# Two fused layers on one core: block 2's loads and score tiles, the value weights' place, and a new written order

## The chip, the cores and the metric

The kernel runs on one core of one Trainium2 chip. The metric is the device time of one execution in microseconds (us), from three runs. A core has TensorE (PE, matmuls; its weight loads are the row PEld), VectorE (DVE), ScalarE (ACT), GpSimd (POOL) and SyncE (SP). They run side by side, each its own instructions in the order written, and wait for each other by semaphores. Data moves by DMAs, which an engine issues and 16 DMA engines carry out.

## What is computed

```python
# first layer: q, k, v are (4 batches, 8 heads, 768 tokens, 64)
for t in range(S):
    state = gamma[h] * state + einsum('bhd,bhe->bhde', k[:, :, t], v[:, :, t])
    y[:, :, t] = scale * einsum('bhd,bhde->bhe', q[:, :, t], state)
# second layer: x is y as (4, 768, 512); x_prev is x one token earlier, zero at the start
xk = mu_k * x + (1 - mu_k) * x_prev
xr = mu_r * x + (1 - mu_r) * x_prev
k = maximum(xk @ w_k, 0)             # w_k (512, 1024)
v = k * k @ w_v                      # w_v (1024, 512)
out = v / (1 + exp(-(xr @ w_r)))     # w_r (512, 512)
```

## The kernel before

**Blocks.** The 3072 tokens are 12 blocks n of 256 tokens, three to a batch. Within a block the recurrence is done as attention: scores of the block's queries with its own keys, masked, times the values, plus the queries times the state that the blocks before left. Powers of gamma are folded into the values (`vs`), the state's decay (`G`) and a table `gy` by which the result is scaled.

**The order is written out by hand.** `ORDER` (L24) is a string of some 635 words, and L753 to L767 turn each word into instructions. A word is a code, its numbers (block first), `@` the PSUM banks that it uses, and `~` the engine: `v` DVE, `a` ACT, `p` POOL, `s` SP; without one it is a PE step. Each engine runs its own words in the order of the string. The words that matter here:

- `lq`, `lk`, `lv` load q, k, v of a block (L221). On POOL's queue they are cast to f16 for q and k. A split load (L227) is two DMAs. `wk.h`, `wv.h` load half of a weight matrix, `wr` the whole of w_r. `cq`, `ck` cast the first four heads of block 0, which SP's queue brings as f32.
- `gy.0`, `gy.1` build the table (L714; DVE). `cm` makes five constant masks: the identity for the transposes, two for 64-row score tiles, two others (L673).
- `Tq`, `Tk` transpose q and k on PE (L271 for blocks 0 to 3); `Eq`, `Ek` copy them out of PSUM. `S` makes scores, `M` masks them (L353, DVE), `C` the state's new part, `U` adds it up (L418), `G` decays it, `I` and `J` multiply queries by the state (L440), `Y` scores by values, `D` scales the result into xT (L513).
- `t` (ACT) and `X` (DVE, L551 for block 0) mix each token with its forerunner; `dx` is the difference that `X` uses for other blocks. `X.n.0.*` is for w_k, `X.n.1.*` for w_r.
- `K` are the matmuls with w_k (L581, L571), `Qa` and `Qb` relu and square (ACT), `R` those with w_r (L611), `s` the sigmoid, `V` those with w_v (L623), `O` the product, `st` the store. `Vc`, `Oc`, `sc` do the last 128 tokens in two halves (L641, L648).
- `z.12` is three f32 matmuls on zeros (L701), `z.1` and `z.2` one and two f16 ones of 128x512 (L708). Nothing reads their result.

**Three ways to make scores.** Blocks 6 to 11 (`HALF`) use 64-token tiles. Blocks in `WIDE` use tiles of 64 rows by 128 columns: `S` is 8 matmuls for each half of the tokens (L330), `Y` 16 (L477), with the `J` part apart, and `C` 8 for a batch's last block (L383). The others use 64x64 tiles: 16 for each half (L338), 32 and the `J` part inside `Y` (L488), 16 for `C` (L394). k and v of `WIDE` and `HALF` blocks are loaded split, since those take token p beside token p+128; the others take tokens 2p and 2p+1, which lie side by side in memory.

Of the kernel before, what the change touches and what calls it, by code (L numbers as in the profile page):

```python
# [12 lines left out]
ALU = mybir.AluOpType  # L13
# [70 lines left out]
def kernel(  # L84
# [12 lines left out]
    nc = tc.nc  # L97
    B, H, S, D = q.shape
# [3 lines left out]
    C = 128  # L102
# [99 lines left out]
    def wide(n):  # L202
        return n in WIDE

# [465 lines left out]
        for m in (1 << l for l in range(7)):  # L670
            nc.vector.tensor_scalar_add(out=count[:, m : 2 * m], in0=count[:, 0:m], scalar1=float(m))

    def masks(e):  # L673
        for out, col, op in (
            (ident, 0, ALU.is_equal), (causal[:, 0], 1, ALU.is_ge), (causal[:, 1], 1, ALU.is_gt),
            (step, 2, ALU.is_ge), (below, 0, ALU.is_ge),
        ):
            nc.vector.tensor_scalar(
                out=out, in0=count[:, 0 : out.shape[-1]], scalar1=mark[:, col : col + 1], scalar2=None, op0=op
            )  # L680

# [56 lines left out]
    def load_wv(e, h):  # L738
# [59 lines left out]
```

## Time and profile before

| what | value |
|---|---|
| median of 3 runs | 154.19 us (154.06 to 155.18) |
| the profiled execution | 154.38 us |
| its span, first to last instruction | 152.6 us |
| busy: PE, DVE, ACT, POOL | 144.1, 128.7, 100.6, 55.3 us |
| moved by DMA | 22.16 MB |

The page's first parts give busy times and, in 40 slices of 3.8 us, busy tenths (9 is 90% or more); PEclk is the clock that TensorE was granted. The chain follows the work that ended last back to the start; in order of time, its columns are start, duration, engine, tile, line and count. In the timeline a row is start, duration, engine, line, operation, output and input, count, and in brackets how long the engine was idle before and what released it. In the table by stretches, each engine has busy time and count.

### The profile page before, as it was taken

How to read it: one execution, taken by the hardware profiler on the slowest of the kernel's cores; microseconds unless marked ns; L12 is line 12 of the kernel's file. 1: busy time of each engine (PE TensorE's matmuls, PEld its weight loads, DVE VectorE, ACT ScalarE, POOL GpSimd, SP SyncE). 2: the span in 40 equal slices, each digit the busy share in tenths (PEclk: the TensorE clock that was granted, in tenths of full speed). 3: DMA queues.
4: the chain of work that ended last, by engine and by line, in shares of the span. 5: the costliest groups of instructions: out<-in, count | busy, mean ns of one | idle time of the engine just before them, and what ended most of it. 6: DMA issues, size and time to landing. Idle time of an engine off the chain costs nothing.

```text
span 152.6 us, 5532 instructions
## 1 busy us (share of the span) xinstructions
PE 144.1 (94%) x2426; PEld 82.9 (54%) x2426; DVE 128.7 (84%) x214; ACT 100.6 (66%) x187; POOL 55.3 (36%) x65
## 2 busy tenths in 40 slices
PE   7977799999999999999999999899999999999990
PEld 3354487758655554547554655557555445744450
DVE  7876999999999999999999999999789999702240
ACT  3466979899934894979483889879405048997130
POOL 7954988579867109997600000000000000000000
PEclk9999999999999999999999999999999999999999
DMA  5999999999999999999999203220002050010435
GB/s 137 215 224 200 207 229 194 170 249 210 196 167 207 236 250 112 290 275 203 206 191 225 83 0 136 81 73 0 4 4 75 0 205 1 14 54 4 158 117 206
DMA packets 45624, 22.16 MB, mean 145 GB/s; under 512 B 37400, under 2 KB 41248, under 8 KB 45600
## 3 DMA queue, kind: packets, MB, share of 16 engines
q0 software_dynamic: 38704, 14.42, 74.0%
q1 hardware_dynamic: 6592, 7.21, 13.7%
q8 instruction: 19, 0.31, 0.8%
q10 hardware_dynamic: 304, 0.18, 0.5%
q14 instruction: 5, 0.04, 0.1%
HBM read 24.16 MB, written 6.29 MB: 200 GB/s over the span
## 4 chain that ended last, share of the span: by engine, by line
PE 91%; DVE 3%; ACT 2%; issue 1%; DVEq 0%
PE ps L623 27%; PE ps L581 14%; PE ps L611 14%; PE ps L571 14%; PE ps L701 4%; PE ps L277 3%; PE ps L440 2%; PE ps L271 2%; DVE a L353 2%; PE ps L330 1%; PE ps L477 1%; ACT qT L240 1%; PE ps L317 1%; PE ps L461 1%; PE ps L641 1%; PE ps L365 1%
## 5 line engine op out<-in xcount | busy, mean ns | idle before, releaser
L623 PE MATMUL ps<-wv,k2s 128*128 128x512 f16 x184 | 43.3, 380 | 0.0
L590 ACT ACTIVATE kr<-ps 128x512 f32<-128x512 f32 x48 | 27.4, 596 | 21.5 <-PE ps L581 11.1
L623 PEld LDWEIGHTS <-k2s 128*128 128x128 f16 x184 | 17.0, 98 | 19.3 <-ACT k2s L602 0.2
L629 DVE SCALAR_TENSOR_TENSOR os<-ps,rs 128x512 f32<-128x512 f32 x23 | 15.5, 685 | 12.4 <-ACT rs L617 7.1
L611 PE MATMUL ps<-wr,xr 128*128 128x512 f16 x96 | 23.5, 379 | 0.0
L581 PE MATMUL ps<-xk,wk 128*128 128x256 f16 x192 | 23.4, 273 | 0.0
L571 PE MATMUL ps<-xk,wk 128*128 128x512 f16 x96 | 22.9, 379 | 0.0
L229 POOL DMA_DIRECT2D k<-in_k_dram x20 | 17.9, 908 | 11.1 <-PE ps L383 6.8
L581 PEld LDWEIGHTS <-wk 128*128 128x128 f16 x192 | 18.3, 98 | 4.4 <-issue 0.2
L240 ACT COPY qT<-ps 128x1024 f16<-128x1024 f16 (+1 forms) x13 | 12.4, 951 | 9.2 <-PE ps L277 7.8
L557 DVE SCALAR_TENSOR_TENSOR xr<-dx,mu,xT 128x256 f16<-128x256 f32 (+1 forms) x32 | 18.0, 579 | 0.1
L617 ACT ACTIVATE rs<-ps 128x512 f32<-128x512 f32 x24 | 13.7, 594 | 6.1 <-DVE os L629 3.2
L229 POOL DMA_DIRECT2D v<-in_v_dram x18 | 16.0, 904 | 3.6 <-DMA wr<-in_moe_w_r_dram 1.9
L557 DVE SCALAR_TENSOR_TENSOR xk<-dx,mu,xT 128x256 f16<-128x256 f32 (+1 forms) x32 | 17.1, 581 | 0.2
L353 DVE TENSOR_TENSOR a<-ps,c_sb 128x1024 f16<-128x1024 f32 (+1 forms) x14 | 14.6, 1066 | 0.7 <-PE ps L338 0.4
L602 ACT ACTIVATE k2s<-kr 128x512 f16<-128x512 f32 x24 | 14.6, 626 | 0.2
L571 PEld LDWEIGHTS <-wk 128*128 128x128 f16 x96 | 9.1, 98 | 10.3
L611 PEld LDWEIGHTS <-xr 128*128 128x128 f16 x96 | 9.1, 98 | 10.2 <-DVE xr L557 0.3
L598 ACT ACTIVATE k2s<-kr 128x512 f16<-128x512 f32 x24 | 14.4, 625 | 0.3
L240 ACT COPY kT<-ps 128x1024 f16<-128x1024 f16 (+1 forms) x13 | 12.3, 944 | 2.9 <-PE ps L271 2.0
L528 DVE TENSOR_TENSOR dx<-xT 128x1024 f32<-128x1024 f32 x11 | 13.5, 1223 | 0.3
L252 DVE TENSOR_TENSOR vs<-v,csm_sb 128x1024 f16<-128x1024 f32 x10 | 12.2, 1219 | 0.2 <-DMA v<-in_v_dram 0.2
(74 smaller groups left out, 165.5 us busy)
## 6 DMA issues: line engine op xcount, KB each, us to landing
out_dram<-os SPq DMA_DIRECT2D x23, 256.0 KB, 3.0
v<-in_v_dram POOLq DMA_DIRECT2D x18, 256.0 KB, 7.3
q<-in_q_dram POOLq DMA_DIRECT2D x11, 256.0 KB, 7.8
k<-in_k_dram POOLq DMA_DIRECT2D x21, 128.0 KB, 8.9
v<-in_v_dram POOLq DMA_DIRECT2D x2, 512.0 KB, 7.1
wk<-in_moe_w_k_dram POOLq DMA_DIRECT2D x2, 512.0 KB, 11.2
wv<-in_moe_w_v_dram POOLq DMA_DIRECT2D x2, 512.0 KB, 9.7
wr<-in_moe_w_r_dram POOLq DMA_DIRECT2D x1, 512.0 KB, 9.3
```

The lines of the kernel that those rows point to most:

```text
L229: e.dma_start(out=dst[:, :, i * D : i * D + D], in_=src[:, i * P : i * P + P].rearrange("h p d -> p h d"),)
L240: e.copy(out=out, in_=in_)
L353: nc.vector.tensor_tensor(out=a_full(n)[:, i, :, j0:j1], in0=pairs(banks("S", n, i, j0))[:, :, j0:j1], in1=(below if wide(n) else causal[: ...
L557: nc.vector.scalar_tensor_tensor(out=XM[w](k)[:, j, t0:t1], in0=DX(k)[:, j, t0:t1], scalar=mu[:, w * NCO + j : w * NCO + j + 1], in1=x[:, ...
L571: nc.tensor.matmul(banks("K", n, g), lhsT=wk16[:, co, g * P : g * P + P], rhs=XM[0](k)[:, co, :], start=(co == 0), stop=(co == NCO - 1),)
L581: nc.tensor.matmul(pz[:, i, :], lhsT=wk16[:, co, fo * P : fo * P + P], rhs=XM[0](k)[:, co, m * TM + t0 : m * TM + t1], start=(i == 0 and c ...
L590: nc.scalar.activation(out=kr, in_=banks("K", n, g, *u), func=AF.Relu)
L598: nc.scalar.activation(out=k2s[:, n % 3 : n % 3 + 2, g, :], in_=kr, func=AF.Square,)
L602: nc.scalar.activation(out=K2(n)[:, w * g : w * g + w, t0:t1], in_=kr.rearrange("p a t -> p (a t)").rearrange("p (i t) -> p i t", i=w), fu ...
L611: nc.tensor.matmul(banks("R", n, tb), lhsT=XM[1](k)[:, co, t : t + P], rhs=wr16[:, co, :], start=(co == 0), stop=(co == NCO - 1),)
L623: nc.tensor.matmul(banks("V", n, tb), lhsT=K2(n)[:, fo, tb * P : tb * P + P], rhs=wv16[:, fo, :], start=(fo == 0), stop=(fo == NFO - 1),)
L629: nc.vector.scalar_tensor_tensor(out=OS(2 * n + tb), in0=banks("V", n, tb), scalar=1.0 / (KSC * KSC), in1=RS(2 * n + tb), op0=ALU.mult, op ...
```

## The change

- `WIDE` loses block 2, so that its k and v are one DMA each, with its scores, values and state in 64x64 tiles, and `J.2` goes into `Y.2`.
- `masks` takes a part, so that the five masks can be placed in three words.
- `ORDER` is another. At the start: `gy.0` stands before the masks; `cq`, `ck` and `Ek.0.2.4` move from ACT to DVE, `U.0.0` from DVE to ACT; `lq.2` moves ahead of `wk.0`, and `wk.1` behind `vs.1` on POOL; `z.12 z.1 z.2` stay of `z.12 z.1` and five `z.2`; `Tq.2` comes ahead of the first `K`. Further on: `wv.0 wv.1` stand ahead of the loads of block 3, `vs.3` is on DVE where it was on POOL, `G.10` on ACT where it was on DVE, and PE's small steps stand in other groups between its large ones. Both orders end with `Vc.11.1.0 Oc.11.1.0 sc.11.1.0`.

```diff
-WIDE = (2, 3, 4, 5)
+WIDE = (3, 4, 5)
 ORDER = """
-cm gy.0~v mu~a lv.0~p lq.0.0.2~s lk.0.0.2~s ck.0.0.2~a cq.0.0.2~a z.12@6 Tq.0.0.2@0 Tk.0.0.2@1 gy.1~v
-z.1@2 mt@2 Ek.0.0.2~a Eq.0.0.2~a S.0.1.0.2@01 S.0.0.0.2@45 me~a lk.0.2.4~p Tk.0.2.4@2 Ek.0.2.4~a
-lq.0.2.4~p vs.0~v C.0@67 U.0.0~v Tq.0.2.4@3 Eq.0.2.4~a lq.1~p lk.1~p M.0.1.0.2~v z.2@2 S.0.1.2.4@23
-U.0.1~v lv.1~p lk.2~p I.0@01 S.0.0.2.4@67 M.0.0.2.4~v wk.0~p wk.1~p G.0~a z.2@6 Tq.1@6 Eq.1~a vs.1~p
-lq.2~p Tk.1@7 Ek.1~a M.0.0.0.2~v M.0.1.2.4~v Y.0 D.0~v t.0.0.3~a t.0.0.2~a t.0.0.1~a lv.2~p z.2@4
-S.1.1@23 M.1.1~v C.1@01 U.1.0~v z.2@4 I.1@23 S.1.0@67 X.0.0.1~v t.0.1.2~a X.0.0.2~v Tk.2@0 t.0.1.3~a
-t.0.0.0~a M.1.0~v X.0.0.0~v z.2@4 Y.1 t.0.1.1~a X.0.0.3~v Ek.2~a K.0.0@0 K.0.1@6 lq.4~p U.1.1~v
-G.1~a wr~p lk.4~p D.1~v dx.1~v X.1.0.2~v X.1.0.0~v K.0.2@1 Qa.0.0~a Qb.0.0~a Qa.0.2~a lq.3~p
...
-lq.11~p Tq.11@67 Ek.11~a X.8.1.2~v Tq.9@45 Eq.9~a K.6.1@0 Qa.6.1~a Eq.11~a R.6.0@2 s.6.0~a K.6.7@4
...
+lv.0~p lk.0.2.4~p mu~a gy.0~v cm.2~v lq.0.2.4~p lq.0.0.2~s cq.0.0.2~v cm.0~v z.12@6 Tq.0.0.2@0
+Eq.0.0.2~a lk.0.0.2~s ck.0.0.2~v Tk.0.0.2@1 Ek.0.0.2~a mt@0 S.0.0.0.2@23 cm.1~v Tk.0.2.4@1 lq.1~p
+vs.0~v C.0@45 gy.1~v Tq.0.2.4@6 Eq.0.2.4~a M.0.0.0.2~v me~a U.0.0~a Ek.0.2.4~v U.0.1~v G.0~a
+S.0.1.0.2@23 M.0.1.0.2~v lk.1~p lv.1~p S.0.0.2.4@67 Tq.1@4 Eq.1~a I.0@01 S.0.1.2.4@23 lk.2~p lq.2~p
+M.0.0.2.4~v Tk.1@5 M.0.1.2.4~v Y.0 D.0~v Ek.1~a t.0.0.3~a S.1.0@23 wk.0~p M.1.0~v vs.1~p Tk.2@5
+C.1@01 U.1.0~v z.1@6 I.1@23 t.0.1.1~a Ek.2~a X.0.0.3~v t.0.0.2~a t.0.0.1~a t.0.0.0~a U.1.1~v
+S.1.1@67 M.1.1~v X.0.0.0~v X.0.0.1~v G.1~a X.0.0.2~v wk.1~p Tq.2@5 t.0.1.0~a Eq.2~a z.2@4 Y.1 D.1~v
+dx.1~v X.1.0.2~v X.1.0.1~v t.0.1.2~a K.0.1@6 Qa.0.1~a t.0.1.3~a Qb.0.1~a K.0.0@7 Qa.0.0~a K.0.2@6
+X.1.0.0~v Qa.0.2~a Qb.0.2~a K.0.3@2 Qa.0.3~a lv.2~p S.2.1@45 lq.4~p X.1.0.3~v K.1.3@6 Qa.1.3~a
+vs.2~v S.2.0@23 Tq.4@01 X.1.1.0~v X.1.1.2~v C.2@7 U.2.0~v X.1.1.1~v wr~p K.1.2@6 Eq.4~a K.1.1@7
+Qa.1.2~a X.1.1.3~v lk.4~p M.2.1~v M.2.0~v I.2@01 R.1.0@6 s.1.0~a R.1.1@4 Qb.0.0~a K.1.0@6 wv.0~p Y.2
+X.0.1.2~v wv.1~p Tk.4@23 X.0.1.3~v Qa.1.0~a X.0.1.0~v Qb.0.3~a Qb.1.0~a X.0.1.1~v R.0.1@6 R.0.0@5
+lv.3~p D.2~v dx.2~v X.2.1.0~v X.2.0.2~v X.2.0.0~v X.2.0.1~v Qb.1.2~a s.0.0~a V.0.0.0@0 V.0.1.0@5
...
-    def masks(e):
+    def masks(e, part):
         for out, col, op in (
-            (ident, 0, ALU.is_equal), (causal[:, 0], 1, ALU.is_ge), (causal[:, 1], 1, ALU.is_gt),
-            (step, 2, ALU.is_ge), (below, 0, ALU.is_ge),
-        ):
-            nc.vector.tensor_scalar(
+            ((ident, 0, ALU.is_equal),),
+            ((causal[:, 0], 1, ALU.is_ge), (causal[:, 1], 1, ALU.is_gt)),
+            ((step, 2, ALU.is_ge), (below, 0, ALU.is_ge)),
+        )[part]:
+            e.tensor_scalar(
```

More of the change, by code (lines that the diff above doesn't have):

```diff
@@ new lines @@
+X.1.0.0~v Qa.0.2~a Qb.0.2~a K.0.3@2 Qa.0.3~a lv.2~p S.2.1@45 lq.4~p X.1.0.3~v K.1.3@6 Qa.1.3~a
[3 more added lines that the diff above has]
+lv.3~p D.2~v dx.2~v X.2.1.0~v X.2.0.2~v X.2.0.0~v X.2.0.1~v Qb.1.2~a s.0.0~a V.0.0.0@0 V.0.1.0@5
+Qa.1.1~a Qb.1.3~a s.0.1~a X.2.0.3~v V.0.1.1 O.0.1~v Ek.4~a lk.3~p K.2.2@1 V.0.0.1 vs.3~v X.2.1.1~v
@@ new lines @@
+Tk.7@23 V.1.1.0@5 V.1.1.1 V.2.0.1 X.3.0.3~v Ek.7~a G.4~a U.5.0~v st.0.0~s O.2.0~v O.2.1~v X.3.1.3~v
+K.3.1@2 K.3.0@4 Ek.5~a S.5.1@01 S.5.0@67 Qa.3.1~a Qa.3.0~a lq.9~p I.5@23 K.3.4@4 Qa.3.4~a lv.7~p
+Qb.3.0~a O.1.1~v lk.6~p K.3.6@5 Qa.3.6~a K.3.3@4 M.5.1~v J.5 Qb.3.1~a Qa.3.3~a M.5.0~v Tk.6@67
+Ek.6~a S.7@01 K.3.7@5 lq.6~p lv.6~p X.3.1.2~v X.3.1.0~v st.2.1~s Qb.3.4~a K.3.2@4 X.3.1.1~v Qb.3.6~a
+Qa.3.7~a Qa.3.2~a M.7~v R.4.1@6 s.4.1~a K.3.5@0 vs.6~v Qb.3.3~a C.6@45 Tq.6@67 vs.7~v Y.5 D.5~v
+U.6.0~a U.6.1~v U.6.2~v U.6.3~v Qa.3.5~a Qb.3.5~a Qb.3.2~a Qb.3.7~a R.3.1@1 dx.5~v X.5.1.3~v
@@ new lines @@
+X.5.0.1~v lv.11~s st.1.1~s R.3.0@0 s.3.0~a V.3.1.0@2 V.3.1.1 s.3.1~a O.3.1~v V.4.1.0@1 V.4.1.1
+X.5.1.2~v G.6~a X.5.0.2~v X.5.0.0~v Eq.6~a I.6@23 C.7@67 S.6@45 M.6~v X.5.0.3~v lq.8~p V.3.0.0@0
+U.7.0~v U.7.1~v V.3.0.1 O.3.0~v K.5.3@4 Qa.5.3~a K.5.1@5 X.5.1.0~v U.7.2~v Qa.5.1~a K.5.2@0 Qa.5.2~a
+Qb.5.2~a I.7@45 X.5.1.1~v Y.6 st.3.0~s st.2.0~s O.4.1~v K.5.0@6 Qa.5.0~a Qb.5.0~a U.7.3~v R.4.0@7
+s.4.0~a D.6~v dx.6~v R.5.1@6 s.5.1~a Qb.5.1~a lq.10~p Tq.10@23 lv.8~p vs.8~v Y.7 D.7~v dx.7~v
+X.6.1.1~v G.7~a Qb.5.3~a X.6.0.3~v X.6.0.2~v X.6.0.0~v lk.8~p Tk.8@01 Ek.8~a Eq.10~a V.5.1.0@6
@@ L80 @@
+X.11.1.0~v R.10.0@3 Qb.9.5~a Qa.11.0~a X.11.1.2~v R.9.1@1 R.11.0@2 Qb.9.6~a Qa.9.7~a st.7.0~s
+Qb.9.7~a s.9.0~a V.9.0.0@4 V.9.0.1 O.9.0~v V.10.1.1 V.9.1.0@6 Qb.11.0~a s.9.1~a Qb.11.1~a V.9.1.1
+O.9.1~v st.9.1~s st.9.0~s s.10.1~a O.10.1~v st.10.1~s R.11.1@4 Qa.11.2~a Qb.11.2~a s.11.1~a
+Vc.11.1.1@7 Oc.11.1.1~v V.11.0.0@4 V.11.0.1 sc.11.1.1~a s.10.0~a V.10.0.0@5 s.11.0~a O.11.0~v
+st.11.0~s V.10.0.1 O.10.0~v st.10.0~s Vc.11.1.0@2 Oc.11.1.0~v sc.11.1.0~s
 """
```

70 lines of the change are left out of this document (24 added, 46 removed).

## The prediction

> **What bounds the kernel now.** I read the page's first parts, then the chain of waits in order of time, then the timeline of the first 21 us and the loads.
>
> ```profile
> span 152.6 us, 5532 instructions
> ...
> PE 144.1 (94%) x2426; PEld 82.9 (54%) x2426; DVE 128.7 (84%) x214; ACT 100.6 (66%) x187; POOL 55.3 (36%) x65
> ...
> PE   7977799999999999999999999899999999999990
> ...
> DVE  7876999999999999999999999999789999702240
> ...
> PEclk9999999999999999999999999999999999999999
> DMA  5999999999999999999999203220002050010435
> ...
> PE 91%; DVE 3%; ACT 2%; issue 1%; DVEq 0%
> ```
>
> The reader is to see three things. PE's row is full from the sixth slice (19 us) to the end, so after 19 us only PE's own work and its few waits count. Ahead of that it shows 7s: this is the only stretch with time to win by order alone. DVE is also full from the sixth slice on, and the DMA engines up to 84 us, so PE's cover is thin there on both sides.
>
> ```profile
> 15.11 0.45 PE ps L338 x16
> ...
> 17.92 1.15 DVE a L353
> ...
> 19.11 0.64 PE ps L488 x32
> ...
> 19.86 3.60 PE ps L581 x32
> ...
> 26.26 0.55 PE ps L330 x16
> ...
> 29.15 0.59 PE ps L477 x16
> ...
> 53.24 0.97 PE ps L623 x4
> ...
> 58.56 0.86 PE ps L623 x4
> ...
> 95.67 0.45 issue
> ...
> 115.57 5.29 PE ps L623 x24
> ...
> 148.57 0.42 DVE os L648
> ```
>
> In this chain (start, duration, work) everything from 19.86 to 148.55 is PE, except 0.45 us of issue at 95.67, in the middle of a run of 64x64 transposes. 24 large matmuls take 5.29 us, 0.22 each. After small tiles a group of four takes 0.97 in place of 0.86, so each return from small to large costs 0.11; I take the same for going there.
>
> So the time is: the moment at which the first `K` can run (19.8 now), PE's work from there, PE's waits, and a tail (`Oc`, the last store) that both orders share. I cost each.
>
> **The first K.** These rows carry the walk.
>
> ```profile
> 3.11 1.62 DVE L678 TENSOR_SCALAR c_sb<-os,csm_sb 128x128 f16<-128x128 f32 x5
> ...
> 4.19 0.56 DVE L716 COPY gy_sb<-csm_sb 128x4 f32<-128x4 f32 x1
> ...
> 4.68 0.62 ACT L240 CAST k<-k2s 128x512 f16<-128x512 f32 x1 [2.01 <-DMA k2s<-in_k_dram]
> 4.78 2.57 DVE L726 TENSOR_TENSOR gy_sb<-gy_sb,csm_sb 128x4 f32<-128x4 f32 x8
> ...
> 7.53 1.23 DVE L252 TENSOR_TENSOR vs<-v,csm_sb 128x1024 f16<-128x1024 f32 x1 [0.18 <-DMA v<-in_v_dram]
> ...
> 9.44 0.42 DVE L242 CAST tg<-ps 128x256 f16<-128x256 f32 x1 [0.68 <-PE ps L394]
> ...
> 9.78 0.68 DVE L353 TENSOR_TENSOR a<-ps,c_sb 128x512 f16<-128x512 f32 x1
> ...
> 12.45 0.64 PE L271 MATMUL ps<-c_sb,q 128*64 128x128 f16 x16
> ...
> 13.58 1.90 POOL L252 TENSOR_TENSOR vs<-v,csm_sb 128x1024 f16<-128x1024 f32 x1 [3.90 <-DMA v<-in_v_dram]
> ...
> 14.26 1.23 DVE L513 TENSOR_TENSOR xT<-ps,gy_sb 128x1024 f32<-128x1024 f32 x1 [1.19 <-PE ps L440]
> ...
> 17.05 0.87 DVE L551 SCALAR_TENSOR_TENSOR xk<-xT,mu,dx 128x256 f16<-128x256 f32 x2
> ```
>
> DVE is free for its first new word at 3.11, as now. `gy.0` comes first: the rows from 4.19 to 7.35 are the copy and eight powers, 3.16 us, and the largest power, about 0.7, is `gy.1`; so `gy.0` takes 2.5, to 5.6. `cm.2` is two of the five masks that took 1.62, 0.6, to 6.2. The casts `cq`, `ck` are new on DVE. No row shows one from SBUF to SBUF: between 0.25 (half of what ACT takes, for a copy that no PSUM slows) and 0.7 (twice the 128x256 cast); I take 0.4, near that 0.42 row, since the source is SBUF. `cq` ends at 6.6, `cm.0` (the identity) at 6.9, and `Tq` starts there. Eight transposes take 0.4; ACT's two copies of 128x512 end near 8.45; the first `S` starts at 8.5. On DVE `ck`, `cm.1` end at 7.9; `vs.0`, whose load lands just ahead of its row's 7.53, at 9.1; `gy.1` at 9.75, the first `M` (0.65) at 10.4, `Ek.0.2.4` (0.55, as an `M`, bounded by 0.4 and 0.7) at 10.95. `U.0.1` waits for ACT's `U.0.0`, which stands behind `C.0` (9.55), `Tq.0.2.4`, its copy and `me`: 11.25. `U.0.1` ends at 11.65, three `M`s at 13.55, `Y.0` (0.64 and the state's part) at 14.4, `D.0` at 15.65, where it ends at 15.49 now.
>
> Behind `D.0` DVE does two large `M` (1.15 each), two `U` (0.35) and four `X` (0.4) before the first `K` may run; now it does the same but one `U`. That gives 20.3 against 19.8. With the short casts, masks of 0.2 and no wait of `U.0.1` it is 19.7; with the long casts, another copy of 0.7 and ACT late for `U.0.0` it is 21.2. I take 20.3. `C.1` hangs on POOL's `vs.1` at 13.58 to 15.48, whose load keeps its place in the queue, and is in time for `U.1.0` at 16.8.
>
> **PE's work from there.** `Tq.2` (0.64 by the row of 16) is done ahead of the first `K`, where it stands behind it now: -0.6. Block 2: `S` is 32 matmuls by the row of 16 in 0.45, 0.9, for 0.55: +0.35. `Y.2` is 0.64 for 0.59, and the eight `J` matmuls stay: +0.05. `C.2` is 16 small ones for 8: between 0 and +0.1, I take 0. Large matmuls are the same in number and shape. I count 25 groups of small steps between large ones from the first `K` on, for 24: +0.2. Sum 0.0. The removed `z.2` lie in idle time ahead of the first `K` and give nothing by themselves.
>
> **PE's waits.** The 0.45 at 95.67 falls in `Tk.11 Tq.11 Tq.9`, 96 transposes in one run; the new order has no run of three `T` so late. I count it as gone, between 0 and -0.45, and a new one is possible at any burst.
>
> **The loads.**
>
> ```profile
> 8.12 1.56 POOL L733 DMA_DIRECT2D wk<-in_moe_w_k_dram  x2
> ```
> ```profile
> wk<-in_moe_w_k_dram POOLq DMA_DIRECT2D x1, 512.0 KB, 10.3
> ```
> ```profile
> 19.75 1.83 POOL L229 DMA_DIRECT2D k<-in_k_dram  x2
> ...
> 30.61 0.78 POOL L740 DMA_DIRECT2D wv<-in_moe_w_v_dram  x1
> 31.76 0.75 POOL L740 DMA_DIRECT2D wv<-in_moe_w_v_dram  x1 [0.37 <-DMA q<-in_q_dram]
> ```
> ```profile
> k<-in_k_dram POOLq DMA_DIRECT2D x2, 128.0 KB, 9.4
> ```
> ```profile
> wv<-in_moe_w_v_dram POOLq DMA_DIRECT2D x1, 512.0 KB, 10.4
> ```
>
> `wk.0` lands at 18.4 now. `lq.2` ahead of it adds one load, and `k.2` as one DMA saves one issue, so about 18.7, against a need at 20.3. `wk.1` is issued behind `vs.1` at 15.5, just behind in the queue, lands near 21, and is needed by the third `K` at 22.1. Ahead of `wv.0` stand the same loads as ahead of `k.4`'s end now, which is at 30.1 (20.7 and 9.4). `wv.1` lands at 42.2 now (31.8 and 10.4); two halves there take about 2.5 each, so here they land near 32.5 and 35. From 20.3, eight `K` (0.9), four `R` and the small steps put `V.0.0.0` at 33.7 and the first use of `wv.1` at 35.5. `v.3` then lands near 37, when DVE reaches `vs.3`; `k.3`, `q.3` near 39 and 40, when PE reaches them. All just in time: cost 0 with little spare. `vs.3` on DVE is 1.2 us more there; its cover is `V.0.*` (four by 0.86), which PE now has ahead of `S.4`. With that cover gone it costs 1.2.
>
> **The sum.** Against the profiled execution: 154.38 + 0.5 (first `K`) + 0.0 (PE's work) - 0.45 (issue) = 154.43. The median of the three runs is 0.19 below that execution, so I predict 154.3: no change.
>
> **The rivals.**
>
> First, *the loads of block 3 come late* (slower). `vs.3` is in DVE's order, ahead of `X.2.1`, `O.0.0` and `M.4`; where `v.3` lands late, all of these wait, and PE soon after, since DVE has nothing spare:
>
> ```profile
> 8.00:12.00 4.00, 2.84 (x87) 1.93 (x87) 2.93 (x6) 2.59 (x9) 1.68 (x3) 1.00 1.61 241
> 12.00:16.00 4.00, 3.63 (x121) 2.33 (x121) 2.72 (x4) 2.35 (x4) 2.42 (x2) 1.00 1.70 188
> 16.00:20.00 4.00, 3.05 (x86) 1.87 (x87) 4.00 (x8) 3.38 (x8) 4.00 (x6) 1.00 1.37 202
> ...
> 36.00:40.00 4.00, 4.00 (x61) 3.20 (x58) 4.00 (x4) 3.94 (x8) 4.00 (x4) 1.00 1.25 206
> ```
>
> The columns are the stretch, its length, PE, PEld, DVE, ACT, POOL, clock and DMA. Two halves of `wv` ahead are 5 us of queue; I found about no spare, so being 1 to 3 us out costs 1 to 3. It decides from about 1.5 late. For it: DMA is full here. Against: `k.2` in larger pieces frees the queue a little. 155.4 to 157.4, say 156.4. Chance 0.24.
>
> Second, *the granted clock falls in the start* (slower). Eight of eleven f16 zero matmuls go. By my walk PE is busy some 3.1, 3.3 and 3.3 us of the three stretches above, against 2.84, 3.63 and 3.05, with no gap over 1 us; but it is small tiles now, and no row shows the clock without the zeros. If it is half from about 12 on, the small steps on the chain (`Y.0`, `S`, `I`, some 2 us) and the first `K`s (3.6 us) take up to twice as long: +2 to +5, say 157.5. It decides as soon as one slice from 4 to 7 has PEclk under 9. Chance 0.14. [...]
>
> Third, *the start is short and PE turns faster* (faster). The walk's lower end puts the first `K` at 19.7, -0.6. The other thing an order can change is what PE pays at the 25 groups: 0.11 going and 0.11 coming back. If tiles that follow each other better spared half of the returns (12 by 0.11), that is -1.3, and 154.3 - 0.6 - 1.3 = 152.4 at best; the first part alone gives 153.7. It needs nearly all of both to decide. For it: the new order has fewer long runs of small tiles. Against: as many groups as before. Chance 0.12.
>
> That the change does nothing of weight is the forecast itself.
>
> **How the numbers follow.** The forecast has 0.50, the late loads 0.24, the clock 0.14, the faster order 0.12. A difference of 1% (1.5 us) is about what a measurement of this kernel tells from no change. Faster by that: 0.12, the third. Slower: the clock 0.14, four fifths of the late loads 0.19 and the forecast's own upper end (first `K` at 21.2 with a new wait) 0.07, in all 0.40. Within: 0.48. The likeliest case alone runs from 153.5 to 155.3. The range takes in the better half of the faster order and the late loads and leaves out the worst of the clock: 152.9 to 157.4.
>
> **What would show it.** In the profile after: the first `K` (L582) within 19.7 to 21.2, `D.0` near 15.7, all PEclk 9; `vs.3` on DVE with no idle time ahead of it; no wait for a weight over 0.5; and L338 with 96 matmuls for 64, L330 with 48 for 64. PEclk under 9, DVE idle ahead of `vs.3`, or more than 2 us of PE waits after 21 us would make me wrong.

## The result, and the profile after

The changed kernel is slower: a median of 162.0 us (159.7 to 164.2, six runs) against 153.96 us of the kernel before on the same chip (153.78 to 155.18, six runs), a ratio of 1.045 with a 95% interval of 1.036 to 1.053. A ratio leaves out the runs that are more than 1.5% above the fastest of the same kernel, and a median counts all of them. The forecast was 154.3, and its range ended at 157.4. The profiled execution took 161.62 us. These are parts of its page that answer to those shown of before.

```profile
span 159.8 us, 5594 instructions
...
PE 147.5 (92%) x2458; PEld 85.3 (53%) x2458; DVE 130.9 (82%) x217; ACT 99.8 (62%) x188; POOL 51.7 (32%) x62
...
PE   7989879999999999992899979999999999999991
...
PEclk9987999999999999999569999999999999999999
...
PE 76%; DMA 10%; DVE 4%; ACT 4%; issue 2%; SPq 1%; ACTq 1%; DVEq 0%
```

PE's row has a hole in the 19th slice (a 2; 72 to 76 us), the granted clock is under 9 in two places (the third and fourth slice, and the two behind the hole), and the chain, which was 91% PE, now has 10% of DMA. The hole is read first, from the chain of waits in order of time (start, duration, what):

```profile
66.05 1.15 DVE vs L252
...
67.22 0.39 SPq L229
...
68.28 7.56 DMA out_dram<-os
...
75.97 0.70 DVE os L629
```

and from SP's waits (line, what it waited for: us in all, times, longest):

```profile
SPq L229 <- DVE vs L252: 8.5, 1, 8.5
```

SP's words here are `lv.11 st.1.1`. `lv.11` writes the buffer that `vs.7` (DVE, 66.05) still reads, so SP stands at it for 8.5 us, and `st.1.1`, whose data had long been ready, stands behind it. It is issued at 68.28, after the two loads of 256 KB, and lands 7.56 us later. `O.3.1` needs the output buffer that this store empties: there are four (`OS`, L152). In the order before, `lv.11` stands behind `st.3.1` (L57), and `st.1.1` goes out at 61.2; the list of changes ahead of the prediction does not have this move. What the late landing did to the engines, from the timeline:

```profile
75.97 0.69 DVE L629 SCALAR_TENSOR_TENSOR os<-ps,rs 128x512 f32<-128x512 f32 x1 [3.79 <-DMA out_dram<-os]
...
76.72 0.33 PE L440 MATMUL ps<-qT,tg 64*64 64x64 f16 x8 [3.70 <-DVE os L629]
...
77.93 3.60 PE L623 MATMUL ps<-wv,k2s 128*128 128x512 f16 x8
```

DVE, and through its PSUM bank PE, waits 3.7 us, and then eight `V` take 3.60 us where eight take 1.90 in the timeline of before: the clock has fallen.

```profile
93.45 1.90 PE L623 MATMUL ps<-wv,k2s 128*128 128x512 f16 x8
```

The table by stretches (length, busy and count of PE, PEld, DVE, ACT, POOL, then clock, DMA share, GB/s) shows it in both places:

```profile
72.00:76.00 4.00, 1.02 (x6) 0.33 (x5) 0.21 (x2) 0.35 (x1) 0.00 (x0) 0.94 1.38 281
76.00:80.00 4.00, 3.28 (x79) 1.88 (x79) 3.80 (x7) 0.00 (x0) 2.16 (x3) 0.50 0.66 45
...
10.00:12.00 2.00, 1.79 (x40) 1.46 (x41) 1.51 (x4) 1.51 (x8) 0.00 (x0) 0.67 1.33 303
12.00:14.00 2.00, 2.00 (x52) 1.66 (x52) 1.11 (x2) 1.74 (x4) 0.12 (x1) 0.50 1.73 188
```

In the trace's clock records, the half clock lasts 3.41 us from 10.67 and 6.83 us from 75.53, which is twice as long (and 10.24 us, three times, in a run below).

The start and the other waits, from the timeline and the chain:

```profile
14.49 1.23 DVE L513 TENSOR_TENSOR xT<-ps,gy_sb 128x1024 f32<-128x1024 f32 x1 [1.29 <-PE ps L440]
...
15.73 0.81 POOL L734 DMA_DIRECT2D wk<-in_moe_w_k_dram  x1
...
19.84 2.19 PE L581 MATMUL ps<-xk,wk 128*128 128x256 f16 x16
...
22.77 1.48 PE L581 MATMUL ps<-xk,wk 128*128 128x256 f16 x12 [0.74 <-DMA wk<-in_moe_w_k_dram]
```
```profile
15.73 6.99 DMA wk<-in_moe_w_k_dram
```
```profile
93.70 0.85 issue
```

The first `K` is at 19.84 (before: 19.79). PE's last instruction ends 7.7 us later than before (156.26 for 148.54), in four parts: 0.74 for `wk.1`, 3.70 for the store, about 2.6 of half clock behind that (an estimate; the eight `V` alone are 1.7 of it), and 0.4 more of issue wait (0.85 for 0.45); 0.3 is left, small steps. The tail behind PE is 0.5 shorter (3.6 for 4.1), which makes the span's 7.2.

### The profile page after: what moved, and what is told of

It is laid out like the page before. It is cut to its first block, busy times and chain, and to the rows that moved or that the text cites. A ratio compares the mean times of both kernels' runs of the same rounds, so it can differ in the third digit from the quotient of the medians.

```text
span 159.8 us, 5594 instructions
## 1 busy us (share of the span) xinstructions
PE 147.5 (92%) x2458; PEld 85.3 (53%) x2458; DVE 130.9 (82%) x217; ACT 99.8 (62%) x188; POOL 51.7 (32%) x62
## 4 chain that ended last, share of the span: by engine, by line
PE 76%; DMA 10%; DVE 4%; ACT 4%; issue 2%; SPq 1%; ACTq 1%; DVEq 0%
PE ps L623 21%; PE ps L571 13%; PE ps L581 12%; PE ps L611 12%; DMA out_dram<-os 6%; DMA wk<-in_moe_w_k_dram 4%; PE ps L702 3%; PE ps L277 3%; PE ps L440 3%; PE ps L271 2%; DVE os L629 1%; PE ps L317 1%; PE ps L365 1%; PE ps L461 1%; ACT rs L617 1%
## 5 line engine op out<-in xcount | busy, mean ns | idle before, releaser
L623 PE MATMUL ps<-wv,k2s 128*128 128x512 f16 x184 | 44.4, 390 | 0.0
L590 ACT ACTIVATE kr<-ps 128x512 f32<-128x512 f32 x48 | 28.0, 598 | 20.9 <-PE ps L581 13.4
L629 DVE SCALAR_TENSOR_TENSOR os<-ps,rs 128x512 f32<-128x512 f32 x23 | 15.5, 685 | 15.9 <-PE ps L623 10.4
L623 PEld LDWEIGHTS <-k2s 128*128 128x128 f16 x184 | 17.6, 100 | 20.3 <-issue 1.6
L617 ACT ACTIVATE rs<-ps 128x512 f32<-128x512 f32 x24 | 14.1, 595 | 20.3 <-DVE os L629 9.2
L581 PE MATMUL ps<-xk,wk 128*128 128x256 f16 x192 | 24.0, 276 | 0.9 <-DMA wk<-in_moe_w_k_dram 0.7
L571 PE MATMUL ps<-xk,wk 128*128 128x512 f16 x96 | 22.3, 379 | 0.0
L229 POOL DMA_DIRECT2D k<-in_k_dram x18 | 16.0, 907 | 8.1 <-PE ps L365 6.1
L229 POOL DMA_DIRECT2D v<-in_v_dram x16 | 14.4, 918 | 5.1 <-DMA wv<-in_moe_w_v_dram 3.5
L234 POOL DMA_DIRECT2D q<-in_q_dram x12 | 10.7, 891 | 16.6 <-PE ps L277 7.8
L252 DVE TENSOR_TENSOR vs<-v,csm_sb 128x1024 f16<-128x1024 f32 x11 | 13.3, 1215 | 0.1
```

Source lines behind the costliest of these rows:

```text
L229: e.dma_start(out=dst[:, :, i * D : i * D + D], in_=src[:, i * P : i * P + P].rearrange("h p d -> p h d"),)
L571: nc.tensor.matmul(banks("K", n, g), lhsT=wk16[:, co, g * P : g * P + P], rhs=XM[0](k)[:, co, :], start=(co == 0), stop=(co == NCO - 1),)
L581: nc.tensor.matmul(pz[:, i, :], lhsT=wk16[:, co, fo * P : fo * P + P], rhs=XM[0](k)[:, co, m * TM + t0 : m * TM + t1], start=(i == 0 and c ...
L590: nc.scalar.activation(out=kr, in_=banks("K", n, g, *u), func=AF.Relu)
L617: nc.scalar.activation(out=RS(2 * n + tb), in_=banks("R", n, tb), func=AF.Sigmoid, scale=1.0 / KSC)
L623: nc.tensor.matmul(banks("V", n, tb), lhsT=K2(n)[:, fo, tb * P : tb * P + P], rhs=wv16[:, fo, :], start=(fo == 0), stop=(fo == NFO - 1),)
```

## The experiments

Kernels marked "on the change" edit the changed kernel, those marked "on before" the kernel before. Ratios are to the kernel before on the same chip.

### The store

**The store ahead of the load** (on the change; the other kernels on the change named below with "the store ahead" contain this edit):

```diff
-X.5.0.1~v lv.11~s st.1.1~s R.3.0@0
+X.5.0.1~v st.1.1~s lv.11~s R.3.0@0
```

> One edit to the changed kernel: on SP's queue st.1.1 stands ahead of lv.11. Theory A: the changed kernel loses 3.7 us because st.1.1 stands behind lv.11, which waits until 67.2 us for vs.7, and then behind lv.11's data (it lands after 7.56 us, at 75.8), so that O.3.1, which needs the buffer, holds DVE and PE to 76; the granted clock then falls to half for 6.8 us, some 2.6 us more. With the store first, O.3.1 does not wait and the clock stays: 161.9 - 6.3 = 155.6 us, PEclk 9 after slice 5. Rival B: the DMA engines are so full at 68 to 76 us that stores land late wherever they stand: over 160 us, DVE still waits for out_dram. Rival C: DVE is behind by its own work there and the store only shows last: 158 to 160 us.

Measured: 156.76 us (155.91 to 158.03), ratio 1.015 (1.010 to 1.020). That is 5.2 us less by the medians and 4.6 by the ratios, from two words on one queue. SP's timeline, the clock's row on the page and two of PE's waits:

```profile
59.84 1.59 SPq L636 DMA_DIRECT2D out_dram<-os  x2
68.74 1.02 SPq L229 DMA_DIRECT2D v<-in_v_dram  x2
```
```profile
PEclk9955799999999999999999999999999999999999
```
```profile
PE ps L365 <- issue: 1.4, 1, 1.4
...
PE ps L277 <- issue: 0.6, 1, 0.6
```

Now both stores go before SP stands still, PE has no wait for a store, and the clock keeps full speed from there on: the fall at 76 followed from the wait. `st.1.1` is issued at 61.10 here and lands at 68.80 by the trace's landing records: 7.70 us with no load ahead of it on the queue. So it is not faster than in the changed kernel, only 7 us earlier. What is left over lies in the start, where this execution waited 1.97 us for the identity (to 7.44), ran at half clock for 10.24 us from 7.66 and reached the first `K` at 21.46, and in two issue waits, 0.64 at 68.36 and 1.35 at 89.56, where the changed kernel has one of 0.85. The 5.2 add up by that: 3.7 for the wait and 2.6 for the clock behind it, less 1.1 for the longer issue waits.

**A small load ahead of the store** (on the change; the loads of `lv.11` on SP bring only the first head of eight, so block 11's values are partly old data):

```diff
+            if split and n == NBLK - 1 and e is nc.sync:
+                hs = slice(0, 1)
             src = x[b, hs, t0 : t0 + TM, :]
```

> The changed kernel with lv.11 on SP's queue loading one head of eight (so block 11's values are partly old ones); its place, its wait for vs.7 and the order of st.1.1 behind it stay. Theory A1: of the store's delay the part that matters is lv.11's data ahead of it on the same queue: st.1.1 is still issued near 68.3 us but lands in 2 to 4 us, before O.3.1 is reached at 72: no DVE wait, no fall of the clock at 76, about 155.6 us. Theory A2: being issued as late as 68.3 is enough by itself: DVE still waits, over 159 us. Rival B (the other queues fill the DMA engines): the store still takes over 6 us, over 160 us.

Measured: 157.59 us (156.84 to 158.41), ratio 1.021 (1.017 to 1.026). The timeline:

```profile
75.63 0.69 DVE L631 SCALAR_TENSOR_TENSOR os<-ps,rs 128x512 f32<-128x512 f32 x1 [1.84 <-DMA out_dram<-os]
76.38 0.26 PE L442 MATMUL ps<-qT,tg 64*64 64x64 f16 x8 [1.74 <-DVE os L631]
```
```profile
69.35 6.16 DMA out_dram<-os
```

The wait is halved, 1.84 for 3.79, but the store still takes 6.16 us with an eighth of the data ahead of it, so the loads' data is at most 1.4 of the 7.56. Even that is not shown: in the run with zeros, next, the whole loads stand ahead and the store lands in 4.59 (69.66 to 74.25). What makes it late is that SP stands at `vs.7` for 8.5 us and issues it at 68.3 to 69.7 in place of 61. Why it then takes between 4.6 and 7.7 us, where the median of the stores is 2.3, is only argued: by the trace's packets POOL's loads moved 0.27 MB meanwhile in the execution of 4.59, and 0.80 to 0.99 MB in the three of 6.16 to 7.70. A wait of 1.74 did not make the clock fall behind it; one of 3.70 did. Length alone does not decide: in later runs it fell behind a wait of 3.00 and not behind one of 3.14.

**Zeros in the wait** (on the change; four f32 zero matmuls, eight records of PE in the trace, where PE waits for the store):

```diff
-G.6~a X.5.0.2~v X.5.0.0~v Eq.6~a I.6@23
+G.6~a X.5.0.2~v X.5.0.0~v Eq.6~a z.16@4 I.6@23
```

> The changed kernel with z.16 (four f32 matmuls on zeros, bank 4) ahead of I.6, that is in the 3.7 us in which PE waits for O.3.1. Theory A: the wait stays, but the granted clock does not fall at 75.5 us, so that the large matmuls after it take 0.22 us and not 0.44: 2 to 3 us less than the changed kernel, 159.2 us. Rival D: the half clock is hidden behind DVE and ACT, which have their own backlog after the wait: under 1 us less, 161 to 162 us.

Measured: 160.86 us (160.68 to 162.13), ratio 1.044 (1.040 to 1.049): in the total no difference that can be told from the changed kernel's. `O.3.1` in the timeline, and the stretches:

```profile
74.41 0.68 DVE L629 SCALAR_TENSOR_TENSOR os<-ps,rs 128x512 f32<-128x512 f32 x1
```
```profile
72.00:76.00 4.00, 4.00 (x18) 1.96 (x17) 3.95 (x8) 2.67 (x7) 2.06 (x3) 1.00 1.31 243
76.00:80.00 4.00, 4.00 (x87) 1.89 (x86) 0.79 (x2) 0.00 (x0) 0.59 (x1) 1.00 1.08 79
```

In this execution `O.3.1` did not wait for the store; the zeros themselves held PE, for 3.43 us, about as long as the wait of 3.70 that they were to fill. The clock holds behind them (1.00 for 0.50), and from the first `K` to PE's end it is 134.15 us for 136.42: 2.3 us less, although the issue waits are 0.7 longer (0.78 and 0.79 for 0.85). Less the 0.3 by which the zeros are shorter than the wait, that makes some 2.7 for the fall of the clock, near the estimate above. The total hides it, since this execution's start ran at half clock for 6.83 us and reached the first `K` at 21.30. The mean granted clock also differs from run to run (0.964 to 0.979 in these four); the next runs take up the start.

### The start

**Zeros back in the start** (on the change, with the store ahead; nine f16 zero matmuls, in groups of one and two, in PE's idle time before the first `K`):

```diff
-Ek.0.0.2~a mt@0 S.0.0.0.2@23
+Ek.0.0.2~a mt@0 z.1@7 S.0.0.0.2@23
-gy.1~v Tq.0.2.4@6 Eq.0.2.4~a
+gy.1~v Tq.0.2.4@6 z.2@7 Eq.0.2.4~a
-M.0.0.2.4~v Tk.1@5
+M.0.0.2.4~v z.2@5 Tk.1@5
-Y.0 D.0~v Ek.1~a
+Y.0 D.0~v z.2@4 Ek.1~a
-C.1@01 U.1.0~v z.1@6 I.1@23
+z.2@4 C.1@01 U.1.0~v z.1@6 I.1@23
```

> The changed kernel with st.1.1 ahead of lv.11, and with nine more f16 matmuls on zeros (z.1 and four z.2) in PE's idle time ahead of the first K. Theory G: the clock stays at full from 7 us on, the first K starts near 20 and not at 21.5, 1 to 1.5 us less than with the store first alone (156.8): 155.5 us. Rival H: the first K hangs on DVE's chain from csm_sb, and is late by that load: within 0.3 us of 156.8, with PEclk all 9.

Measured: 155.38 us (154.35 to 156.56), ratio 1.008 (1.005 to 1.011). The page's clock row, and PE's longest wait after the first `K`:

```profile
PEclk9999999999999999999999999999999999999999
```
```profile
PE ps L365 <- issue: 1.1, 1, 1.1
```

Work that computes nothing took 1.4 us off by the medians, 1.1 by the ratios. The mean granted clock is 0.995 to 1.0 in every run, where it was 0.967 to 1.0 without these zeros, and the first `K` is at 19.89. Not all of the 1.4 is the clock, though: with nine more matmuls ahead, the issue waits of 0.64 and 1.35 have become one of 1.10, which is 0.9 less, and the one run without these zeros that had the full clock took 156.01. The runs do not separate the two.

**The kernel before without its small zeros** (on before; all five `z.2` ahead of the first `K` removed, the rest of the order as it was):

```diff
-M.0.1.0.2~v z.2@2 S.0.1.2.4@23
+M.0.1.0.2~v S.0.1.2.4@23
...
-M.1.0~v X.0.0.0~v z.2@4 Y.1
+M.1.0~v X.0.0.0~v Y.1
```

> The kernel before without its five z.2 words (ten f16 matmuls on zeros that nothing reads); its order is otherwise as it was. Theory G: these hold the granted clock while PE has only small tiles to do; without them PEclk falls under 9 in slices 2 to 5 for 3.4 us or more, PE's small steps on the chain take up to twice as long, and the first K starts 0.5 to 1.7 us later: 155.0 to 156.0 us. Rival H: the clock stays, or its fall is hidden behind DVE and the loads: within 0.3% of before.

Measured: 157.65 us (155.25 to 159.38), ratio 1.015 (1.010 to 1.019); by the medians it is 2.2%. Time follows the granted clock: 0.989 with 155.25, 0.977 with 156.72, 0.963 with 157.33, and 0.966 to 0.968 with the three that took longest (157.96 to 159.38). The issue wait is as before (0.41 for 0.45). Page and stretches of the fastest:

```profile
PEclk9999779999999999999999999999999999999999
```
```profile
12.00:16.00 4.00, 2.70 (x115) 2.24 (x114) 3.15 (x5) 2.58 (x5) 2.41 (x2) 1.00 1.69 193
16.00:20.00 4.00, 2.83 (x81) 2.46 (x81) 4.00 (x8) 3.45 (x8) 4.00 (x6) 0.67 1.38 203
```

PE is busy 2.70 us from 12 to 16, where the prediction's row of before has 3.63, and from the first transposes to the first `K` no wait of PE is longer than 0.8. From 16 to 20 the clock is 0.67, where before has 1.00. So the clock falls without any long gap, and it is the zeros that held it: 0.963 to 0.989 in the runs without them, 0.995 to 1.0 in the runs of before beside them. How much work is enough can't be read off: before has only 2.84 us from 8 to 12 and keeps its clock (1.00).

**wk.1 early** (on the change, with the store ahead):

```diff
-S.1.0@23 wk.0~p M.1.0~v vs.1~p Tk.2@5
+S.1.0@23 wk.0~p wk.1~p M.1.0~v vs.1~p Tk.2@5
-G.1~a X.0.0.2~v wk.1~p Tq.2@5
+G.1~a X.0.0.2~v Tq.2@5
```

> As the kernel with the store first, and on POOL's queue wk.1 stands ahead of vs.1 and not behind it. Theory E: wk.1 is 1.7 us later than I predicted (issued 15.7, landed 22.7) because a load through POOL takes some 7 us from issue to landing even where the queue has run dry, not because the queue is full; issued near 9 it lands by 20.5 and K.0.2 waits for no load: 0.7 to 1.0 us less than with the store first, 154.7 us. Rival F: the queue is full, so what wk.1 gains the loads behind it lose: K.0.2 does not wait, but the difference is within 0.3 us.

Measured: 157.67 us (156.59 to 157.89), ratio 1.020 (1.017 to 1.024): no gain over 156.76. The timeline:

```profile
23.97 1.25 PE L581 MATMUL ps<-xk,wk 128*128 128x256 f16 x10 [0.66 <-ACT kr L590]
```

The wait for `wk.1` is gone and another of the same length stands in its place. `K.0.2` writes bank 6, which `Qa.0.1` must have read, and `Qa.0.1` stands on ACT behind `t.0.1.2`, which waits for `D.1`. The two waits ended together, and the expectation saw only the one that the changed kernel's profile names; the profile with the store ahead had already named the other (0.67 behind ACT).

**Both of them away** (on the change, with the store ahead, the zeros and wk.1 early):

```diff
-X.1.0.1~v t.0.1.2~a K.0.1@6 Qa.0.1~a t.0.1.3~a
+X.1.0.1~v K.0.1@6 Qa.0.1~a t.0.1.2~a t.0.1.3~a
```

> The changed kernel with the store first and the zeros at the start (155.4), with wk.1 ahead of vs.1 on POOL, and with Qa.0.1 and not t.0.1.2 first on ACT behind D.1. Theory M: K.0.2 had two waits that end at the same time, wk.1's landing (22.7) and its bank, which Qa.0.1 frees only after t.0.1.2 has waited for D.1; removing the load's alone changed nothing, and removing both takes the 0.66 us wait away: 0.5 to 0.8 us less, 154.7 us. Rival N: a third wait (X.1, the other banks) stands at the same place: within 0.3 us of 155.4.

Measured: 154.81 us (154.13 to 156.38, 12 runs), ratio 1.006 (1.004 to 1.009): 0.6 less than with the zeros alone by the medians, but 0.3 by the ratios, whose intervals overlap. The waits of PE:

```profile
PE ps L271 <- DMA k<-in_k_dram: 1.4, 1, 1.4
...
PE ps L365 <- issue: 0.9, 1, 0.9
```

No `K` waits now, so the mechanism is shown; that it is worth 0.6 is not clear of the noise. The first row is new, a load of k that landed late in this execution (its first `K` is at 21.05). This is the best form of the changed order that was run, and the kernel before is still ahead of it by 0.6%.

### Where PE's instructions come from

**Block 2 alone** (on before; `WIDE` without 2, `Y.2` where `J.2` stood):

```diff
-WIDE = (2, 3, 4, 5)
+WIDE = (3, 4, 5)
-Tq.4@01 Eq.4~a Y.2
+Tq.4@01 Eq.4~a
-R.1.1@4 Tk.4@01 Ek.4~a J.2 R.1.0@6
+R.1.1@4 Tk.4@01 Ek.4~a Y.2 R.1.0@6
```

> The kernel before with block 2's part of the change alone: k and v unsplit, 64x64 tiles; Y.2, which then holds J.2, stands where J.2 stood. Theory A: this part costs what I counted, 0.4 us of PE's work (16 S matmuls in 0.45 us against 8 in 0.27, twice, and Y.2), little of it shown: 154.3 to 154.8 us, within 0.3%. Rival: it is what makes the changed kernel slow in part, by another distribution of the loads: over 155.5 us.

Measured: 162.16 us (160.14 to 162.58), ratio 1.047 (1.042 to 1.052). The expectation had nothing of that size. Two of the runs have the full clock (160.14 and 160.23), and the four at 0.987 to 0.989 take 162.09 to 162.58, so some 2 of the 8 us are half clock. The waits of PE in the execution of 160.23:

```profile
PE ps L277 <- issue: 3.5, 2, 2.5
PE ps L571 <- DVE a L346: 1.7, 1, 1.7
```

The 1.7 is a wait for DVE's mask at 54.81; no run explains it. The 3.5 is new: PE stops twice inside bursts of 64x64 transposes and waits for nothing that the profile names. What the trace has at these places is a 16 KB transfer of instructions (the page's row of queues, "q8 instruction", counts 19 with 0.31 MB). In the changed kernel, PE's 2458 weight loads and as many matmuls over 19 transfers are some 259 instructions each, 129 pairs. In all 23 such stops of 0.4 us or more behind the first 15 us, in 13 of the 14 profiles of this case, PE goes on 1.2 to 1.6 us after the end of a transfer; this is read here as a wait for its own instructions.

**Forty tiny matmuls in idle time** (on before; the three f32 zero matmuls of `z.12` become two and forty f16 ones of 128x32, in the idle time before the first transposes, to shift all that follows; the trace counts 38 more pairs of weight load and matmul, since an f32 one makes two; no other word is touched):

```diff
-z.12@6
+z.8.40@6
+        for _ in range(tiny):
+            nc.tensor.matmul(
+                pz[:, 0:32], lhsT=z16[:, 0:P], rhs=z16[:, 0:32], start=True, stop=True,
+                skip_group_check=True,
+            )
```

> The kernel before with one f32 zero matmul fewer at the start and forty tiny ones (128x32, f16, on zeros) in its place, in the time in which PE has nothing to do; all later instructions are the same. In block 2's part alone, forty more pairs of weight load and matmul stand ahead of the later work, and PE waited 3.5 us at 78.7 and 82.9 in the middle of small tiles where before waits 0.45 at 95.7. Theory K: what matters is where the 16 KB transfers of PE's instructions end against the runs of small tiles: here the same shift gives the same waits, 3 to 4 us, 157 to 158 us. Rival L: the waits come of block 2's own work or loads: the time stays within 0.5% of before.

Measured: 162.22 us (160.7 to 163.47), ratio 1.048 (1.043 to 1.054). The chain of waits:

```profile
79.25 0.78 issue
80.02 0.38 PE ps L277 x22
...
83.22 3.00 issue
86.22 0.25 PE ps L277 x6
```

For comparison the chain of the block 2 run:

```profile
78.70 1.01 issue
79.70 0.38 PE ps L277 x24
...
82.88 2.47 issue
85.35 0.26 PE ps L277 x8
```

The same two bursts stop, for about as long, without any change to block 2. Another 2 us lie in an issue wait of 0.92 at 20.02 and a wait of 1.11 for DVE at 36.65 (a mixing step of DVE took 2.27 us there for the usual 0.48, unexplained), and behind the wait of 3.00 the clock is half for 3.41 us. So 3.5 of the 6 us that block 2 cost by itself at full clock are not its work: they are where in PE's stream the transfers fall. In the trace's transfer records the eleventh of the 19 comes late in every kernel, after 187 to 233 pairs without one where mostly 70 to 180 lie between two, and begins near pair 1500: at 83.75 here (pair 1502), 83.15 with block 2 alone (1502), 92.16 in the changed kernel (1485), 80.81 in before (1478). In before it falls on large matmuls (18 in the timeline from 79.67 to 83.72), and none of PE's rows there has a wait; in small tiles, of which 32 last 0.4 us, PE stops, for 3.00 us in one wait.

**Large matmuls ahead of that place** (on the change, with the store ahead and the zeros):

```diff
-s.5.0~a C.8@45 U.8.0~v lq.11~p Tq.8@23
-Eq.8~a V.5.0.0@0 V.5.0.1 st.3.1~s
+s.5.0~a V.5.0.0@0 V.5.0.1 C.8@45 U.8.0~v lq.11~p Tq.8@23
+Eq.8~a st.3.1~s
```

> As the kernel with the zeros at the start, and V.5.0.0 V.5.0.1 (eight large matmuls, 1.7 us) stand ahead of C.8 and Tq.8 and not behind them. Theory I: the 1.35 to 1.57 us of issue wait in the middle of C.8 is PE waiting for its next 16 KB of instructions, which are fetched from 88.1 and are used up at 89.6 because small tiles take 0.01 us each; large matmuls in between cover it: the wait goes under 0.5 us and the time is about 1 us less than with the zeros alone, 154.5 us. Rival J: the wait is for something else in C.8 (the values, the bank): it stays as long, only later.

Measured: 155.53 us (154.96 to 156.32), ratio 1.009 (1.006 to 1.012): no gain over the 155.38. The waits of PE:

```profile
PE ps L623 <- issue: 1.5, 1, 1.5
```

The wait moved into the large matmuls and is 1.52 us, where it was 1.10. That these hide it by being large is not so in general: it failed here.

**A shift by 22 pairs** (on the change, as the best form above; one f32 zero matmul fewer, 24 tiny ones):

```diff
-z.12@6
+z.8.24@6
```

> As the kernel without the second wait, with one f32 zero matmul fewer at the start and 24 tiny ones in its place, which moves all later PE instructions 24 pairs on. Theory K: the wait of 1.1 us in C.8 falls into the large matmuls ahead of it and goes: 1 us less than without the shift, 153.7 us, under before. Rival L: the wait stays in C.8, whatever stands ahead: within 0.3 us.

Measured: 160.99 us (158.21 to 162.8, six runs, which spread over 3%). The waits of PE:

```profile
PE ps L623 <- issue: 3.1, 1, 3.1
```

Neither theory held. The wait moved from small tiles into large matmuls, as a shift may do, but it grew from 0.9 to 3.1. The rest of the 6 us lies in the start: the granted clock is 0.968 to 0.987 in these runs although all twelve f16 zero matmuls are there. In the profile PE waits 1.39 us just ahead of the first transposes, where the run with the zeros has no such wait, the clock is half for 6.83 us from 7.62, and the first `K` is at 22.51. That the count of PE's instructions moves these waits is shown; how long one will be is not something that these runs let one forecast, and why the eleventh transfer comes late stays open.

### The value weights

**wv ahead of block 3's loads, alone** (on before):

```diff
-G.1~a wr~p lk.4~p D.1~v
+G.1~a wr~p lk.4~p wv.0~p wv.1~p D.1~v
```

(and the two words removed where they stood).

> The kernel before with wv.0 and wv.1 right behind lk.4 on POOL's queue, ahead of the loads of block 3. Theory O: block 3's q, k and v land some 5 us later, and its order asks for them near 34 us (q.3 lands at 31.5 before): PE waits 2 to 3 us there, 156 to 157 us. Rival P: DMA has slack by then, or what is late is hidden: within 0.5% of before.

Measured: 159.28 us (158.28 to 160.08), ratio 1.034 (1.030 to 1.037). The timeline of PE:

```profile
36.48 0.64 PE L271 MATMUL ps<-c_sb,q 128*64 128x128 f16 x16 [2.15 <-DMA q<-in_q_dram]
...
38.28 0.58 PE L271 MATMUL ps<-c_sb,k 128*64 128x128 f16 x14 [0.69 <-DMA k<-in_k_dram]
38.79 3.43 PE L581 MATMUL ps<-xk,wk 128*128 128x256 f16 x16
```

In the order before, the weights ahead push block 3's q and k past their need: 2.15 and 0.69 of waiting, and the 16 `K` behind take 3.43 for some 1.9, at half clock (the mean of this execution is 0.989). The changed order has no such wait: its transposes of block 3 run at 40.1 and 40.8, where those of before run at 34.4 and 34.9. The first rival's mechanism is real, and the rest of the order avoids it.

## Why the prediction was wrong

Step by step, in the order of the prediction:

- **The first K.** Forecast 20.3 (19.7 to 21.2), measured 19.84: a term of +0.5 that was 0. `D.0` was forecast to end at 15.65 and ended at 15.72; from there to the first `K` it took 4.1 us for the 4.65 that the walk gave. The steps of the walk were sound (`cq`, 128x512 from SBUF, took 0.41 for 0.4; the 128x256 cast out of PSUM takes 0.42 in before), but that the end came out so near is in part luck: this start ran at half clock for 3.41 us, which the walk had not in it, and DVE was ready for `D.0` 0.35 earlier than the walk had it (13.20 for 13.55). In the other four profiles of the changed order without zeros added in the start the first `K` is at 21.1 to 21.6.
- **PE's work.** Sum 0.0; about 0.3 is what the account above leaves over for it. The counts are as forecast:

```profile
L338 PE MATMUL ps<-qT,kT 64*64 64x128 f16 x96 | 3.1, 229 | 0.7 <-DVE a L353 0.3 <-ACT kT L240 0.3
...
L330 PE MATMUL ps<-qT,kT 64*128 64x128 f16 x48 | 1.9, 217 | 0.0
```

- **"The removed `z.2` lie in idle time ahead of the first `K` and give nothing by themselves."** Wrong. By themselves, taken from the kernel before, they cost 1.5% (1.0 to 1.9), and nine of the same given to the changed order gained 1.4 us, the clock's part of which is not separated from shorter issue waits. The second rival had the mechanism. That the clock would fall to half was the author's estimate: in the profile of before it is full (1.000) over the whole span, and the one after has 0.50, for 3.41 us in the start. Its price of 3.2 (157.5 for 154.3) was high: the runs give 2.2 to 3.5 in the order before and at most 1.4 in the changed one. That the change with the store ahead is at 156.76 is near it by luck, since other waits are in that too. Its chance of 0.14 was too low, because the absence of gaps over 1 us was taken as an argument against it, and that is what fell.
- **The issue wait.** Counted as -0.45, it came back as 0.85 at 93.70. "A new one is possible at any burst" was said and given no price. The runs give it one, up to 3.1 for a single wait, so the bound of 0.45 from the one row of before was far too small; here, by chance, it is 0.4 longer than before, so that the term was 0.85 out.
- **The loads.** The step that failed: "All just in time: cost 0", in a walk of POOL's queue and no other, and a list of PE's waits that has the 0.45 of issue alone. `vs.3` and the value weights came out as forecast: first `V` at 34.26 for 33.7, `vs.3` at 37.73 with no idle time ahead, and the halves of `wv` landed at 32.6 and 35.1 for 32.5 and 35. `wk.1` was issued at 15.73 for 15.5 and landed at 22.7 for "near 21": 0.74 of waiting. The load that mattered was on SP's queue: `lv.11` moved from behind `st.3.1` to ahead of `st.1.1`. It waits 8.5 us for `vs.7`, the store behind it lands 7.56 us after its issue, and with four output buffers `O.3.1` waits for that. That the store would go out late could be read from the two orders: what `lv.11` must wait for, what stands behind it on SP, how many stores ahead the buffers reach. How long it would take to land could not be read there. This step was worth 5.2 us (the two words swapped): 3.7 of wait and some 2.6 of half clock behind it, less 1.1 by which the issue waits were longer with the words swapped.
- **The tail**, "shared by both", is 0.5 shorter than before.

So the 7.8 us between 162.0 and 154.2 (before, beside the later runs) are, by the runs one after the other: 5.2 the store, 1.4 the zeros in the start (the clock, and shorter issue waits), 0.6 the two waits of `K.0.2` (not clear of noise), and 0.6 left, in which the longer issue wait (0.86 for 0.45) lies. The first rival (late loads of block 3) was not what happened, though it would have in the order before. The third had nothing for it: no run shows a gain from PE's turns between tile sizes.

Shown by runs: the store's place, the zeros' hold on the clock in the start (0.995 to 1.0 with them, 0.963 to 0.989 without, in the order of before), that `K.0.2` had two waits, and that a shift of PE's stream alone costs 4.8%. Only argued: that the half clock explains the later first `K` of single profiles (the one with the store ahead also began its DVE work 0.5 late, behind its first load, and its first transposes at 7.44 for 6.56), why the store takes so long to land, and that the place of the transfers is what the remaining 0.6 us is.

## What to carry to other kernels

When an order changes, walk every queue that issues DMAs, SP's too: for each load, what it must wait for, which stores stand behind it, and how many buffers are left until an engine needs one of those stores to have landed. Before a matmul on zeros is counted as nothing, ask whether the clock holds without it: here five words of them were worth 1.5% in the order before. And a difference of a few per cent after an edit to small tiles (4.8% here) can be the place where instruction transfers fall: a run with a few tiny matmuls added in idle time shows how much such a shift does by itself.

## What the runs showed of the hardware that was not expected

- One and the same store of 256 KB took 7.56 us from issue to landing behind two loads of 256 KB on its queue, 6.16 with these cut to one head of eight, 4.59 behind the whole loads in another run, and 7.70 with no load ahead; 2.3 us is the median of the 23 stores in the first of these profiles.
- Without the five `z.2`, the granted clock halves for 3.41 us (in the fastest run) in a start where, from the first transposes on, no wait of PE is longer than 0.8 us, differently from run to run of the same kernel (0.963 to 0.989). In four profiles PE had also waited 1.3 to 2.0 us just ahead of the first transposes, and there it halved for 6.83 or 10.24 us. In the changed order a dozen f16 zero matmuls hold it (0.995 to 1.0 in the seven runs with the zeros), and no longer hold it where one of the f32 ones ahead of the first transposes is replaced by tiny ones (0.968 to 0.987).
- Forty tiny matmuls in idle time cost 8 us elsewhere: the profile has 4.7 us more of PE's stops at transfers of its instructions (3.00 in one burst of 64x64 transposes), and 3.41 us of half clock behind that.
